# Regrouping the first phase of a fused attention and GEGLU kernel: transposes a slot ahead, stores deferred to SP, more buffers, first fills overlapped

## Chip, cores, metric

One core of one Trainium2 chip. The metric is device time of a whole execution in microseconds (us); lower is better. "Faster" or "slower" means by more than 2%. Of one core there are no sister cores to compare with, so a run counts as slow only if it lies 1.5% above the fastest of its kernel; no run quoted with a ratio did, and the state of a single run is unknown. Marks inside an execution are read from its trace, in us from its start.

## The reference, cut to what matters

```python
x = A_x                                            # 1 x 2048 x 1024, bf16
g = sigmoid((x * gate_w).sum(-1, keepdims=True))   # one gate value for each row
# a: 64 segments of 32 rows; each sees 8 memory rows as well; 40 rows in all
for s in range(64):
    h = concat([mem, x[:, 32*s:32*s+32]])
    q, k, v = h @ Wq, h @ Wk, h @ Wv               # 32 heads of 128
    o = softmax(mask(q k^T * scale)) v ;  o = o @ Wo
    mem = o[:, :8]; outs.append(o[:, 8:])           # the first 8 go to the next segment, 32 are output
# b: GEGLU over all rows
b = gelu(x @ w_gate) * (x @ w_up) @ w_down         # 1024 -> 3584 -> 1024
return g * a + (1 - g) * b
```

The 64 segments depend on one another through `mem`. b doesn't depend on them.

## The kernel before

A list of operations is recorded, and each waits on semaphores for what it reads or overwrites. Five engines work: TensorE (PE), ScalarE (ACT), VectorE (DVE), GpSimd (POOL) and SP, which only issues transfers. A transfer belongs to a "lane", a semaphore; two transfers of one lane are issued one after the other's landing.

**First phase.** 16 tiles of x, 128 rows each, are transposed, kept for products with the first four of 28 gate/up column blocks, and stored to scratch for later. Each "slot" has the products of one column block and the transposes of one tile:

```python
xr = al("xr", [128, TB, KC, 4, NB])                # one buffer
def do_x(T):                                       # tile T; a block is 4 tiles, tb = T % 4
    ... 8 transposes of px[T % 4] into PSUM bank 6 + T % 2
    act: two copies  xTp[fb % 2] <- PSUM
    dve: xr[:, tb] <- PSUM                          # last 8 rows of each segment
    pool: gp <- px * gwb ;  dve: dl[:, T] <- sum(gp)
    if tb == TB - 1:                                # at once, on ACT
        op("act", dma xq_scr <- xTp, lane=f"xw{fb % 2}")
        op("act", dma xr_scr <- xr,  lane="xv")
...
more(4)                                             # four weight slots
for T in range(TB): do_x(T); load_x(T + NPX)
for fb in range(NFB):
    for j in range(NJP):
        pre_j(fb, j)                                # 2 x 8 products, gelu; the last also stores g on ACT
        T = TB * (fb + 1) + j
        if T < NT: do_x(T); load_x(T + NPX)
        more(2)                                     # two more weight slots
more(99)
... gal = 1 / (1 + exp(-dl))
for u in range(2):                                  # late slots: their memory was xTp, wgp, gpre ...
    for m in "vo": ... first((m, u, i))
```

**Weights.** 52 SBUF slots of 512 KB hold the 64 pieces into which Wq, Wk, Wv and Wo are cut. Twelve of them are shared by two pieces and are refetched in every segment when the last use is past. All weight loads stand in SP's one order.

**First fills.** "Fills" compute k, q and v of the last 8 rows of four segments at once ("tails"). Eight of them precede or lie inside segment 0:

```python
def fill0(m, u, b, n, G=0, h=hR):
    for f in fill(m, u, b, h): f()                  # 32 products, all 8 pieces of the weight
    fill_evac(m, u, b, stage[n])                    # ACT copies PSUM
    if m != "v": fill_trans(); fill_put(stage[n], "dve")
    fill_store(m, u, G, stage[n])                   # GpSimd: qk_scr (lane "fq") or v_scr
# in segment 0, in the places named:
#   k,0: fill0 k 0, q 0 (G=0), k 0, q 0 (G=1, hR1)   v,0: fill0 v 0
#   v,0 step 4: load_qk(0, 0); rest_k(0); load_v     k,1: fill0 k 1, q 1, v 1; load_qk(0, 1); load_v; load_r(1)
```

load_qk brings the tails of segment 0 back from qk_scr, load_r(1) brings hR for the second group. After segment 0 come 63 more segments and the rest of the GEGLU.

## Time and profile before

| | us |
|---|---|
| median of 4 runs | 2257.8 (2256.4 to 2265.1) |
| span of the trace | 2259.6 |
| first phase over (last gate/up product) | 113.7 |
| last of the first fills ends | 153.9 |
| segment 0 ends (transposes of a_bf) | 175.6 |

The profile page has the busy digits of 40 equal slices of the span; a view by stretches sums each engine's busy time in stretches that one chooses, with the granted TensorE clock (PEclk), the mean busy share of the 16 DMA engines and the GB/s that they moved. A line of waits has: who waited, for whom, us in total, times, the longest. A line of a timeline has: start, duration, engine, line, operation, operands, count, and in brackets the idle time ahead of it and what ended that. The lines themselves are in the prediction.

### The profile page before, as it was taken

Reading aid. Unit: us, or ns where it says so; the run is one execution under the profiler, and the core shown is the slowest. Engines: PE = TensorE matmul, PEld = TensorE weight load, DVE = VectorE, ACT = ScalarE, POOL = GpSimd, SP = SyncE. Lnnn points to the kernel's source line nnn. Section 1 sums busy time; section 2 is a strip of 40 time slices with the busy share of each in tenths; the row PEclk is TensorE's granted clock in tenths of the full one; section 3 lists DMA queues with packets and bytes.
Section 4 is the critical chain, followed back from the end, with each engine's and each line's share of the span. In section 5 each row is a group of like instructions: output and inputs, shape, how many; then the busy total and the mean of one; then the engine's idle time right before and its main releaser. Section 6 shows DMA issues by size and latency. Waiting matters only on the chain.

```text
span 2259.6 us, 80049 instructions
## 1 busy us (share of the span) xinstructions
PE 2083.4 (92%) x36642; PEld 1098.8 (49%) x36642; DVE 905.4 (40%) x2151; ACT 612.1 (27%) x1296; POOL 618.3 (27%) x1138
## 2 busy tenths in 40 slices
PE   6668999999999999999999989999888999999999
PEld 3324455555545555555555545555543444444444
DVE  4523344334334334334334433433434516344362
ACT  3312223223232323323222232322222303122130
POOL 4223332433433243342333334233321000000000
PEclk9889999999999999999999999999999999999999
DMA  8777888788788888778878878888889500100000
GB/s 288 294 267 269 286 288 296 263 297 307 266 281 300 286 284 316 275 269 316 289 266 295 305 258 286 307 280 283 294 285 342 214 28 29 38 24 33 19 29 19
DMA packets 203536, 529.24 MB, mean 234 GB/s; under 512 B 29640, under 2 KB 46664, under 8 KB 203200
## 3 DMA queue, kind: packets, MB, share of 16 engines
q1 hardware_dynamic: 169264, 464.59, 57.5%
q0 software_dynamic: 28992, 51.94, 7.4%
q10 hardware_dynamic: 4944, 7.60, 0.9%
q8 instruction: 287, 4.70, 0.8%
q14 instruction: 49, 0.40, 0.1%
HBM read 490.36 MB, written 33.55 MB: 232 GB/s over the span
## 4 chain that ended last, share of the span: by engine, by line
PE 76%; DMA 12%; POOL 4%; issue 4%; DVE 2%; ACT 1%; SPq 0%; ACTq 0%; DVEq 0%; POOLq 0%
PE pb L734 24%; PE pb L440 16%; PE pb L746 8%; PE pb L1047 7%; PE pb L761 7%; PE pb L646 4%; DMA sl<-in_A_Wo_dram 3%; DMA sl<-in_A_Wv_dram 3%; PE pb L776 3%; DMA a_scr<-a_bf 2%; PE pb L667 2%; DMA xr_scr<-xr 1%; POOL v_scr L802 1%; PE pb L661 1%; DMA sl<-in_A_Wk_dram 1%
## 5 line engine op out<-in xcount | busy, mean ns | idle before, releaser
L734 PE MATMUL pb<-sl,hT 128*32 128x512 bf16 x12288 | 749.4, 382 | 28.0 <-issue 13.8
L734 PEld LDWEIGHTS pb<-sl,hT 128*32 128x32 bf16 x12288 | 331.7, 97 | 294.7 <-issue 26.7
L746 PE MATMUL pb<-sl,oT 128*32 128x256 bf16 x8192 | 280.3, 275 | 48.7 <-issue 42.8
L634 ACT ACTIVATE tok<-pb 128x512 bf16<-128x512 f32 x320 | 191.0, 597 | 414.7 <-PE pb L734 365.0
L719 POOL COPY oRc<-oT 128x128 bf16<-128x128 bf16 x128 | 97.9, 765 | 647.0 <-DVE oT L637 624.0
L746 PEld LDWEIGHTS pb<-sl,oT 128*32 128x32 bf16 x8192 | 207.8, 97 | 96.9 <-issue 53.2
L761 PE MATMUL pb<-sl,hR 128*32 128x512 bf16 x3072 | 228.0, 385 | 7.5 <-DMA hR<-xr_scr 3.0
L440 PE MATMUL pb<-xT,wg 128*128 128x512 bf16 x768 | 182.8, 381 | 4.1 <-DMA wg<-in_B_w_gate_dram 4.1
L440 PE MATMUL pb<-xT,wu 128*128 128x512 bf16 x768 | 181.4, 379 | 0.0
L1047 PE MATMUL pb<-wd,GT 128*128 128x512 bf16 x784 | 169.9, 379 | 0.0
L637 DVE CAST oT<-pb 128x160 bf16<-128x160 f32 x256 | 71.0, 319 | 220.2 <-PE pb L710 219.7
L634 ACT ACTIVATE vA<-pb 128x512 bf16<-128x512 f32 x128 | 76.4, 597 | 273.9 <-PE pb L734 273.9
L428 ACT ACTIVATE s<-pb 128x512 f32<-128x512 f32 x112 | 66.9, 597 | 307.2 <-PE pb L440 307.1
L637 DVE COPY kT<-pb 128x512 bf16<-128x512 bf16 x128 | 51.8, 405 | 233.5 <-PE pb L646 88.8
L646 PE MATMUL pb<-ident,tok 128*128 128x128 bf16 x1280 | 127.6, 222 | 17.4 <-DVE stg L637 5.7
L646 PEld LDWEIGHTS pb<-ident,tok 128*128 128x128 bf16 x1280 | 72.9, 98 | 127.6 <-ACT tok L634 95.4
L429 DVE SCALAR_TENSOR_TENSOR tp<-s,pb 128x512 f32<-128x512 f32 x112 | 76.8, 685 | 133.3 <-ACT s L428 132.9
L672 DVE TENSOR_REDUCE st<-pb 128x8 f32<-128x320 f32 x128 | 62.9, 492 | 148.1 <-PE pb L667 148.1
L440 PEld LDWEIGHTS pb<-xT,wg 128*128 128x128 bf16 x768 | 75.3, 98 | 95.6 <-issue 6.2
L1047 PEld LDWEIGHTS pb<-wd,GT 128*128 128x128 bf16 x784 | 76.7, 98 | 92.5
L440 PEld LDWEIGHTS pb<-xT,wu 128*128 128x128 bf16 x768 | 75.1, 98 | 90.7 <-issue 0.2
L994 POOL DMA_DIRECT2D out_dram<-osb x14 | 7.6, 547 | 372.4 <-PE pb L440 224.6
(86 smaller groups left out, 2149.7 us busy)
## 6 DMA issues: line engine op xcount, KB each, us to landing
sl<-in_A_Wv_dram SPq DMA_DIRECT2D x394, 512.0 KB, 8.8
sl<-in_A_Wo_dram SPq DMA_DIRECT2D x205, 512.0 KB, 6.0
sl<-in_A_Wk_dram SPq DMA_DIRECT2D x142, 512.0 KB, 5.5
sl<-in_A_Wq_dram SPq DMA_DIRECT2D x79, 512.0 KB, 6.8
qk_scr<-stg POOLq DMA_DIRECT2D x64, 128.0 KB, 5.9
qkr<-qk_scr POOLq DMA_DIRECT2D x128, 64.0 KB, 2.2
wd<-in_B_w_down_dram SPq DMA_DIRECT2D x7, 1024.0 KB, 14.6
px<-in_A_x_dram SPq DMA_DIRECT2D x16, 256.0 KB, 5.2
```

The lines of the kernel that those rows point to most:

```text
L428: op("act", lambda e: e.activation(s1[:, :], hg, ACTF.Square, scale=SQ), rd=[BK(bg)], wr=[s1.r()])
L429: op("dve", lambda e: e.scalar_tensor_tensor(out=t[:, :], in0=s1[:, :], scalar=1.0, in1=hg, op0=ALU.add, op1=ALU.mult), rd=[BK(bg), s1.r() ...
L440: ins = e.matmul(PB[bk][:, 0:FB], lhsT=w[:, kc, cc:cc + 128], rhs=x[:, :, :, kc, :].rearrange("p t i c -> p (t i) c"), start=(kc == 0), st ...
L634: op("act", lambda e: e.activation(o, i, ACTF.Copy), rd=rd, wr=wr)
L637: op("dve", lambda e: e.tensor_copy(o, i), rd=rd, wr=wr)
L646: ins = e.transpose(PBV[TT][:, j * 128:(j + 1) * 128], tok[:, j * 128:(j + 1) * 128], ident[:, :])
L719: op("pool", lambda e: e.tensor_copy(oRc[:, u, :, :].rearrange("p c x -> p x c"), oT[:, :, :, 32:40].rearrange("p g j c -> p (g j) c")), r ...
L734: ins = e.matmul(PB[bk][32 * g:32 * g + 32, :], lhsT=h[:, i, :], rhs=w[:, g * 512:(g + 1) * 512], start=(p % 8 == 0), stop=(p % 8 == 7))
L746: ins = e.matmul(PB[XO][32 * g:32 * g + 32, 0:256], lhsT=oT[:, gp_, 2 * jj + hh, 0:32], rhs=w[:, c:c + 256], start=(r == 0 and p % 8 == 0 ...
L761: ins = e.matmul(PB[b][32 * g:32 * g + 32, :], lhsT=h[:, k[2], :], rhs=w[:, g * 512:(g + 1) * 512], start=(n == 0), stop=(n == 7))
L776: ins = e.matmul(PB[b][32 * g:32 * g + 32, 0:256], lhsT=t[:, :, 2 * i + hh], rhs=w[:, c:c + 256], start=(ends[0] and i == 0 and hh == 0), ...
L1047: ins = e.matmul(PB[bank[2 * k + hf]][:, :], lhsT=GT[:, j, tb * 128:(tb + 1) * 128], rhs=w[:, jj, hf * 512:(hf + 1) * 512], start=(j == 0) ...
```

## The change

The intent is to take the stalls out of the first phase and the first fills. Stores are issued a slot later on SP; xr has two buffers; the first gate/up weights are two tiles each, and their second halves are asked for behind two more x tiles; transposes go ahead of the products; three weight slots are asked for at each step instead of two; late slots are asked for as their memory comes free; first fills overlap with one another, and the tails of segment 0 are copied on chip (they are still stored as well, for segments 1 to 3).

```diff
-        wgp = al("wgp", [128, KC, NJP * 128])
+        wgp = [al(f"wgp{h}", [128, KC, NJP * 64]) for h in range(2)]       # wup likewise
-        xr = al("xr", [128, TB, KC, 4, NB])
+        xr = [al(f"xr{i}", [128, TB, KC, 4, NB], at=(cur[0], xr1)[i]) for i in range(2)]
+        tokB = al("tokB", [128, 512], at=oT.off)
+        st0 = stage + [al(f"st0{i}", [128, 512], at=odd0 + 1024 * i) for i in range(2)]
...
             if j == NJP - 1:      # and the xq_scr and xr_scr stores of do_x likewise
-                op("act", lambda e: e.dma_start(g_scr[fb], ...), lane=f"gw{fb % 2}")
+                puts.append(lambda: op("sp", lambda e: e.dma_start(g_scr[fb], ...), lane=f"gw{fb % 2}"))
...
         for fb in range(NFB):
             for j in range(NJP):
-                pre_j(fb, j)
                 T = TB * (fb + 1) + j
+                now, puts[:] = list(puts), []
                 if T < NT:
                     do_x(T)
                     load_x(T + NPX)
-                more(2)
+                more(3)
+                if T >= NT:
+                    more_late(2 if j < 3 and not inits else 0)
+                for f in now:
+                    f()
+                pre_j(fb, j)
...
         def fill(m, u, b, h=hR):
-            ks = [(m, u, i) for i in range(8)]
+            ks = [(m, u, i) for i in range(8) if i not in PAIRS[m]] + [(m, u, i) for i in PAIRS[m]]
...
+        def tr0(m, u, t, n, G=0):
+            op("pe", lambda e: trans4(e, t), ...)
+            fill_put(st0[n], "dve")
+            if G == 0:            # the tail of segment 0, on chip
+                op("pool", lambda e: e.tensor_copy(qkr[:, u, 0 if m == "q" else 1, :], st0[n][:, 0:128]), ...)
+            fill_store(m, u, G, st0[n])
...              # segment 0
-                on("k", 0, 0, lambda: fill0("k", 0, F1, 0))    # ... and the others one by one
+                on("k", 0, 0, lambda: mm0("v", 0, F1, st0[3]))
+                on("k", 0, 0, lambda: mm0("k", 0, F2, tokB))
+                on("q", 0, 0, lambda: mm0("q", 0, F1, tokB), lambda: more_late(4))
+                on("k", 1, 0, fills_1)
+                on("k", 1, 0, lambda: op("dve", lambda e: e.tensor_copy(hR[:, :, :], hR1[:, :, :]), ...))
+                on("k", 1, 0, lambda: (load_v(0, slice(1, 2)), more_late(99)))
```

More of the change, by code (lines that the diff above doesn't have):

```diff
@@ L406, in bass_gated_mix__memory_aug_recurrent_mem_tr__geglu_ffn__prompt_kernel @@
         NPX = min(NT, 4)
-        xTp = [al(f"xTp{i}", [128, TB, 4, KC, SEG]) for i in range(2)]
-        wgp = al("wgp", [128, KC, NJP * 128])
-        wup = al("wup", [128, KC, NJP * 128])
-        gpre = [al(f"gpre{i}", [128, NJP, FB]) for i in range(2)]
         px = [al(f"px{i}", [128, D]) for i in range(NPX)]
+        gp = al("gp", [128, D], FP32)
         pm = al("pm", [128, D])
         gwb = al("gwb", [128, D])
-        gp = al("gp", [128, D], FP32)
-        dl = al("dl", [128, NT], FP32)
+        xTp = [al(f"xTp{i}", [128, TB, 4, KC, SEG]) for i in range(2)]
+        wgp = [al(f"wgp{h}", [128, KC, NJP * 64]) for h in range(2)]
+        wup = [al(f"wup{h}", [128, KC, NJP * 64]) for h in range(2)]
+        gpre = [al(f"gpre{i}", [128, NJP, FB]) for i in range(2)]
         memT = al("memT", [128, 64])
+        xr1 = cur[0]
+        cur[0] += 2 * TB * KC * 4 * NB
         assert cur[0] <= top
@@ L420, in bass_gated_mix__memory_aug_recurrent_mem_tr__geglu_ffn__prompt_kernel @@
         s1 = al("s1", [128, FB], FP32)
-        xr = al("xr", [128, TB, KC, 4, NB])
+        xr = [al(f"xr{i}", [128, TB, KC, 4, NB], at=(cur[0], xr1)[i]) for i in range(2)]
+        cur[0] += xr[0].nb
+        tokB = al("tokB", [128, 512], at=oT.off)
+        st0 = stage + [al(f"st0{i}", [128, 512], at=odd0 + 1024 * i) for i in range(2)]
+        dl = al("dl", [128, NT], FP32, at=stage[1].off + stage[1].nb - 64)
+        assert cur[0] <= dl.off
         hR1 = al("hR1", [128, KC, 32], at=pB.off)
-        assert cur[0] <= pB.off and hR1.nb <= pB.nb
+        assert hR1.nb <= pB.nb
         hT = hTs[0]
@@ L447, in pre_j @@
             for bk, w in ((bg, wgp), (bu, wup)):
-                up(w, xTp[fb % 2], bk, 128 * j)
+                up(w[2 * j // NJP], xTp[fb % 2], bk, 128 * (j % (NJP // 2)))
             g = gpre[fb % 2]
@@ L451, in pre_j @@
             if j == NJP - 1:
-                op("act", lambda e: e.dma_start(g_scr[fb], g[:, :, :].rearrange("p j c -> p (j c)")), rd=[g.r()],
-                   wr=[("D", "g", fb)], lane=f"gw{fb % 2}")
+                puts.append(lambda: op("sp", lambda e: e.dma_start(g_scr[fb], g[:, :, :].rearrange("p j c -> p (j c)")), rd=[g.r()],
+                                       wr=[("D", "g", fb)], lane=f"gw{fb % 2}"))
+        puts = []
         def load_g(fb):
@@ L472, in do_x @@
             x, n = xTp[fb % 2], 4 * KC * SEG
+            xo_ = xr[fb % 2]
             def f(e):
@@ L481, in do_x @@
             op("act", lambda e: e.activation(x[:, tb, 2:4, :, :], pv[:, 2:4], ACTF.Copy), rd=[BK(b)], wr=[x.r(tb * n + n // 2, tb * n + n)])
-            op("dve", lambda e: e.tensor_copy(xr[:, tb, :, :, :], PBV[b].rearrange("p (k i c) -> p k i c", k=KC, i=4)[:, :, :, NR:SEG]),
-               rd=[BK(b)], wr=[xr.r(256 * tb, 256 * tb + 256)])
+            op("dve", lambda e: e.tensor_copy(xo_[:, tb, :, :, :], PBV[b].rearrange("p (k i c) -> p k i c", k=KC, i=4)[:, :, :, NR:SEG]),
+               rd=[BK(b)], wr=[xo_.r(256 * tb, 256 * tb + 256)])
             op("pool", lambda e: e.tensor_tensor(out=gp[:, :], in0=t[:, :], in1=gwb[:, :], op=ALU.mult),
@@ L486, in do_x @@
             if T < 2:
-                op("pool", lambda e: e.tensor_copy((hR, hR1)[T][:, :, :], xr[:, tb, :, :, :].rearrange("p k i c -> p k (i c)")),
-                   rd=[xr.r(256 * tb, 256 * tb + 256)], wr=[(hR, hR1)[T].r()])
+                op("pool", lambda e: e.tensor_copy((hR, hR1)[T][:, :, :], xo_[:, tb, :, :, :].rearrange("p k i c -> p k (i c)")),
+                   rd=[xo_.r(256 * tb, 256 * tb + 256)], wr=[(hR, hR1)[T].r()])
             op("dve", lambda e: e.tensor_reduce(dl[:, T:T + 1], gp[:, :], AX.X, ALU.add), rd=[gp.r()], wr=[dl.r(T, T + 1)])
             if tb == TB - 1:
-                op("act", lambda e: e.dma_start(xq_scr[TB * fb:TB * fb + TB].rearrange("t p i c -> p t (i c)"),
-                                                x[:, :, :, :, :].rearrange("p t i k c -> p t (i k c)")), rd=[x.r()],
-                   wr=[("D", "xq", y) for y in range(TB * fb, TB * fb + TB)], lane=f"xw{fb % 2}")
-                op("act", lambda e: e.dma_start(xr_scr[TB * fb:TB * fb + TB].rearrange("t p c -> p t c"),
-                                                xr[:, :, :, :, :].rearrange("p t k i c -> p t (k i c)")), rd=[xr.r()],
-                   wr=[("D", "xr", y) for y in range(TB * fb, TB * fb + TB)], lane="xv")
+                puts.append(lambda: op("sp", lambda e: e.dma_start(
+                    xq_scr[TB * fb:TB * fb + TB].rearrange("t p i c -> p t (i c)"), x[:, :, :, :, :].rearrange("p t i k c -> p t (i k c)")),
+                    rd=[x.r()], wr=[("D", "xq", y) for y in range(TB * fb, TB * fb + TB)], lane=f"xw{fb % 2}"))
+                puts.append(lambda: op("sp", lambda e: e.dma_start(
+                    xr_scr[TB * fb:TB * fb + TB].rearrange("t p c -> p t c"), xo_[:, :, :, :, :].rearrange("p t k i c -> p t (k i c)")),
+                    rd=[xo_.r()], wr=[("D", "xr", y) for y in range(TB * fb, TB * fb + TB)], lane=f"xv{fb % 2}"))
         def load_h(s):
@@ L522, in bass_gated_mix__memory_aug_recurrent_mem_tr__geglu_ffn__prompt_kernel, with load_pre @@
             load_x(T)
-        for h in range(2):
-            for w, W, nme in ((wgp, B_w_gate, "gp"), (wup, B_w_up, "up")):
+        def load_pre(h):
+            for w, W, nme in ((wgp[h], B_w_gate, "gp"), (wup[h], B_w_up, "up")):
                 c0, c1 = h * NJP * 64, (h + 1) * NJP * 64
-                op("sp", lambda e, w=w, W=W, c0=c0, c1=c1: e.dma_start(w[:, :, c0:c1], W[:, c0:c1].rearrange("(kc p) c -> p kc c", p=128)),
+                op("sp", lambda e, w=w, W=W: e.dma_start(w[:, :, :], W[:, c0:c1].rearrange("(kc p) c -> p kc c", p=128)),
                    wr=[w.r()], lane=f"{nme}{h}")
+        load_pre(0)
         inits = [k for k in [at_step(p, 0) for p in range(24)] + [(m, 1, i) for m in "kqv" for i in range(8)]
@@ L534, in more, with more_late @@
             del inits[:n]
-        more(4)
+        late = [k for k in [(m, u, i) for u in range(2) for m in "vo" for i in range(8)]
+                if home[k] >= spare and uses[home[k]][0] == k]
+        late.sort(key=lambda k: home[k])
+        def more_late(n):
+            for k in late[:n]:
+                first(k)
+            del late[:n]
         op("pe", tr_mem, rd=[pm.r(), ident.r()], wr=[BK(5)])
@@ L545, in bass_gated_mix__memory_aug_recurrent_mem_tr__geglu_ffn__prompt_kernel @@
                    rd=[xTp[0].r(0, KC * SEG)], wr=[hT.r()])
+            if T == 1:
+                load_pre(1)
+        more(4)
         for fb in range(NFB):
             for j in range(NJP):
-                pre_j(fb, j)
                 T = TB * (fb + 1) + j
+                now, puts[:] = list(puts), []
                 if T < NT:
@@ L552, in bass_gated_mix__memory_aug_recurrent_mem_tr__geglu_ffn__prompt_kernel @@
                     load_x(T + NPX)
-                more(2)
-        more(99)
-        op("act", lambda e: e.activation(gal[:, :], dl[:, :], ACTF.Exp, scale=-1.0), rd=[dl.r()], wr=[gal.r()])
-        op("dve", lambda e: e.tensor_scalar(out=dl[:, :], in0=gal[:, :], scalar1=1.0, scalar2=None, op0=ALU.add),
-           rd=[gal.r()], wr=[dl.r()])
-        op("dve", lambda e: e.reciprocal(gal[:, :], dl[:, :]), rd=[dl.r()], wr=[gal.r()])
-        for u in range(2):
-            for m in "vo":
-                for i in range(8):
-                    if home[m, u, i] >= spare:
-                        first((m, u, i))
+                if T == NT:
+                    op("act", lambda e: e.activation(gal[:, :], dl[:, :], ACTF.Exp, scale=-1.0), rd=[dl.r()], wr=[gal.r()])
+                    op("dve", lambda e: e.tensor_scalar(out=dl[:, :], in0=gal[:, :], scalar1=1.0, scalar2=None, op0=ALU.add),
+                       rd=[gal.r()], wr=[dl.r()])
+                    op("dve", lambda e: e.reciprocal(gal[:, :], dl[:, :]), rd=[dl.r()], wr=[gal.r()])
+                more(3)
[4 more added lines that the diff above has]
+                pre_j(fb, j)
+        for f in puts:
+            f()
+        more(99)
+        more_late(8 - len(hosts) + spare + len(late))
         cur[0] = res0
@@ L642, in evac, with trans4 @@
             act_copy(t[:, :], PB[bank][:, :], [BK(bank)], [t.r()])
-        def trans4(e):
+        def trans4(e, t=tok):
             for j in range(4):
-                ins = e.transpose(PBV[TT][:, j * 128:(j + 1) * 128], tok[:, j * 128:(j + 1) * 128], ident[:, :])
+                ins = e.transpose(PBV[TT][:, j * 128:(j + 1) * 128], t[:, j * 128:(j + 1) * 128], ident[:, :])
             return ins
@@ L808, in fill_store, with mm0 @@
                    rd=[st.r()], wr=[("D", "qk", G, m4)], lane="fq")
-        def fill0(m, u, b, n, G=0, h=hR):
+        def mm0(m, u, b, t, G=0, h=hR):
             for f in fill(m, u, b, h):
                 f()
-            fill_evac(m, u, b, stage[n])
-            if m != "v":
-                fill_trans()
-                fill_put(stage[n], "dve")
-            fill_store(m, u, G, stage[n])
+            act_copy(t[:, :], PB[b][:, :], [BK(b)], [t.r()])
+            if m == "v":
+                fill_store(m, u, G, t)
+        def tr0(m, u, t, n, G=0):
+            op("pe", lambda e: trans4(e, t), rd=[t.r(), ident.r()], wr=[BK(TT)])
+            fill_put(st0[n], "dve")
+            if G == 0:
+                x = 256 * u + 128 * (m == "k")
+                op("pool", lambda e: e.tensor_copy(qkr[:, u, 0 if m == "q" else 1, :], st0[n][:, 0:128]), rd=[st0[n].r(0, 128)],
+                   wr=[qkr.r(x, x + 128)])
+            fill_store(m, u, G, st0[n])
         def rest_k(r):
@@ L853, in bass_gated_mix__memory_aug_recurrent_mem_tr__geglu_ffn__prompt_kernel @@
             if s == 0:
-                on("k", 0, 0, lambda: fill0("k", 0, F1, 0))
-                on("q", 0, 0, lambda: fill0("q", 0, F1, 1))
+                on("k", 0, 0, lambda: mm0("v", 0, F1, st0[3]))
+                on("k", 0, 0, lambda: mm0("k", 0, F2, tokB))
                 if NG > 1:
-                    on("k", 0, 0, lambda: fill0("k", 0, F2, 1, 1, hR1))
-                    on("q", 0, 0, lambda: fill0("q", 0, F2, 0, 1, hR1))
-                on("v", 0, 0, lambda: fill0("v", 0, F1, 1))
@@ L860, in bass_gated_mix__memory_aug_recurrent_mem_tr__geglu_ffn__prompt_kernel @@
-                on("v", 0, 4, lambda: (load_qk(0, 0), rest_k(0), load_v(0, slice(0, 1))))
-                on("k", 1, 0, lambda: fill0("k", 1, F1, 0))
-                on("k", 1, 0, lambda: fill0("q", 1, F2, 1))
-                on("k", 1, 0, lambda: fill0("v", 1, F1, 0))
-                on("k", 1, 0, lambda: (load_qk(0, 1), load_v(0, slice(1, 2)), load_r(1) if NG > 1 else None))
+                    on("k", 0, 0, lambda: mm0("k", 0, F1, tok, 1, hR1))
+                    on("k", 0, 4, lambda: tr0("k", 0, tok, 1, 1))
@@ new lines, in bass_gated_mix__memory_aug_recurrent_mem_tr__geglu_ffn__prompt_kernel, with q_next @@
+                on("k", 0, 0, lambda: tr0("k", 0, tokB, 0))
+                on("q", 0, 0, lambda: mm0("q", 0, F1, tokB), lambda: more_late(4))
+                if NG > 1:
+                    def q_next():
+                        for f in fill("q", 0, F2, hR1):
+                            f()
+                        tr0("q", 0, tokB, 2)
+                        act_copy(tokB[:, :], PB[F2][:, :], [BK(F2)], [tokB.r()])
+                    on("q", 0, 0, q_next)
+                    on("q", 0, 3, lambda: tr0("q", 0, tokB, 3, 1))
+                else:
+                    on("q", 0, 3, lambda: tr0("q", 0, tokB, 2))
@@ new lines, in bass_gated_mix__memory_aug_recurrent_mem_tr__geglu_ffn__prompt_kernel, with fills_1 @@
+                on("v", 0, 4, lambda: (rest_k(0), load_v(0, slice(0, 1))))
+                def fills_1():
+                    mm0("k", 1, F1, tok)
+                    for f in fill("q", 1, F2):
+                        f()
+                    tr0("k", 1, tok, 1)
+                    act_copy(tok[:, :], PB[F2][:, :], [BK(F2)], [tok.r()])
+                    mm0("v", 1, F1, st0[2])
+                    tr0("q", 1, tok, 3)
+                on("k", 1, 0, fills_1)
+                if NG > 1:
+                    on("k", 1, 0, lambda: op("dve", lambda e: e.tensor_copy(hR[:, :, :], hR1[:, :, :]), rd=[hR1.r()], wr=[hR.r()]))
```

## The prediction

> **What bounds the kernel now.** I first read the page's 40 slices. TensorE is over 90% busy in nearly every slice after the third, and the change touches nothing there but the order of eight products inside a fill. What can be won lies in the first three or four slices of 56.5 us:
>
> ```profile
> PE   6668999999999999999999989999888999999999
> PEclk9889999999999999999999999999999999999999
> DMA  8777888788788888778878878888889500100000
> ```
>
> Next I asked for the busy times of the stretches that the code suggests. 0 to 113.6 us is the first phase (x transposed, 16 pairs of gate/up products, stores to scratch); 113.6 to 153.8 us ends with the last of the eight first fills; at 175.6 us the first of 64 segments ends (the two transposes of a_bf):
>
> ```profile
> core 0: us, PE busy (x) PEld busy (x) DVE busy (x) ACT busy (x) POOL busy (x), PEclk, DMA share, GB/s
> 0.00:20.00 20.00, 8.98 (x51) 4.90 (x52) 6.04 (x12) 7.40 (x11) 12.43 (x25) 1.00 0.82 255
> 20.00:113.60 93.60, 68.62 (x342) 31.52 (x340) 47.34 (x71) 30.89 (x55) 25.51 (x12) 0.87 0.82 297
> 113.60:153.80 40.20, 26.08 (x386) 10.45 (x385) 5.20 (x12) 5.77 (x11) 7.57 (x12) 0.90 0.94 350
> 153.80:175.60 21.80, 18.75 (x414) 9.22 (x411) 8.16 (x22) 6.76 (x16) 9.58 (x19) 0.87 0.35 106
> 175.60:199.10 23.50, 20.65 (x476) 10.98 (x476) 9.57 (x27) 6.35 (x16) 6.21 (x13) 1.00 0.81 293
> ```
>
> The reader should see two things. TensorE idles and runs under its full clock up to 153.8 us, though a later segment takes only 23.5 us. But the last two columns show the DMA engines 82% and 94% busy, so there is far less slack in transfers than in TensorE. Third, the waits up to 180 us name the stalls of the first phase; fourth, TensorE's timeline shows one of them whole:
>
> ```profile
> DVE xr L482 <- DMA xr_scr<-xr: 19.3, 3, 12.3
> ```
>
> ```profile
> 78.10 1.89 PE L440 MATMUL pb<-xTp,wup 128*128 128x512 bf16 x8
> 86.34 1.03 PE L476 MATMUL pb<-ident,px 128*128 128x128 bf16 x8 [6.35 <-DVE xr L482]
> 90.16 3.59 PE L440 MATMUL pb<-xTp,wgp 128*128 128x512 bf16 x8 [2.79 <-DVE gpre L434]
> 93.55 2.36 PE L440 MATMUL pb<-xTp,wup 128*128 128x512 bf16 x8
> ```
>
> VectorE can't refill the single xr buffer until its store has landed; TensorE then waits for VectorE, cools down, and its next eight products take 3.59 us in place of 1.89.
>
> **What the Trainium skill says.** "TensorE: Matmul & The Clock Gate", "What's actually happening": the array falls to half its clock after an idle window of about 3.4 us. The lines above agree (3.59 against 1.89 us after the gap). "DMA: Bandwidth & Descriptors", "Issuing engines are not separate DMA queues": transfers issued by SP, ACT or GpSimd run on the same 16 engines, and another issuer saves only sequencer time. So moving stores from ACT to SP buys no bandwidth; this trace agrees in so far as share and GB/s rise and fall together whichever queue works. The same page, "Specifications", gives some 358 GB/s of HBM for a core and 435 for the fabric. This trace had 414 GB/s in 72 to 96 us with weights alone, so the measurement decides: the lower figure is not the ceiling here, the upper one is nearly reached.
>
> **The change part by part.**
>
> 1. Two xr buffers, and stores one slot later on SP. This takes away the 19.3 us of VectorE waiting for xr stores, and frees ACT, which held its own copies back behind stores.
>
> 2. Each x tile is transposed a slot before the products that it follows now, and the first weights are in separate halves. The first product waits for half of the weights (SP's waits show the first halves there at 9.9 and 11.4 us), not until 13.8 and 18.9 us. The three waits of TensorE for ACT's xTp copies (11.9 us together) go.
>
> What compute alone would allow: in the good stretches of the first phase VectorE's slot is xr 0.2, dl 1.2, three products 0.7 each and a tanh of 0.65 between: 4.03 us by the timeline (37.05 to 33.02). TensorE's slot is 0.45+2x1.73 = 3.9 us. The first gelu waits for the chain of gp (2.12) and dl (1.21) of tiles 0 to 4, five times about 3.45 after 6.1 us, so it ends near 26 us. Eleven more slots of 4.1 us give 71; then four slots without x at TensorE's 3.46: the first phase would end near 82 to 85 us rather than 113.6.
>
> 3. The first fills. Order is changed, evacuations overlap other fills, and the tails of segment 0 are copied on chip, so that no qk_scr round trip is waited for (4.3 us of GpSimd waiting for qkr); hR for group 1 is a copy (3.0 us of TensorE waiting for hR). Eight fills of 1.74 us are still to be done, and segment 0.
>
> 4. The o and late v slots are asked for as their memory comes free. In the trace SP issues nothing from 88.8 to 113.7 us (its waits: 17.2 us put to an xq_scr store, then 7.7 us to gate/up products that still read the memory), and the DMA engines fall idle: 35 GB/s in 104 to 108 us, 0 in 108 to 112, 77 in 112 to 116.
>
> **Why the sum is not the sum of the waits.** Count the bytes in SP's new order, in MB (a slot is 512 KB, 0.524 MB). Up to about 20 us: the first eight x tiles 2.1, gate/up weights 2.1, gate_w 0.3, others: 4.7. From there to the end of the last fill (v, second half, which needs refetched v slots): x 2.1; 49 first slots 25.7; refetches of 2 k, 1 q and 6 v slots 4.7; four sets of stores of 1.05+0.26+0.52, 7.3; instructions and small scratch transfers some 1.2: **41 MB**. Every one of them is in front of the refetched v slots in SP's queue. Before moved 297x93.6 + 350x40.2 = 41.9 MB for it, in 0.82x93.6+0.94x40.2 = 114.5 us of full DMA share: 0.366 MB per us of busy engine. Weights alone reach 0.414. With share near 1 and somewhat better packets in flight I take 0.383: 41/0.383 = 107 us, so the last fill ends near 20+107 = **127 us**. Compute alone would be there near 103 (85, plus eight fills 14, plus three stages of projection 5). So transfers become the bound, and 127 replaces 153.8.
>
> From there to the end of segment 0 before took 21.8 us. This path stays nearly as it is: four v_scr stores on GpSimd, the wait for them, the load of vB, then pB, and only then the second part of attention (vB's issue came 5.8 us after the last fill before). The hR wait that goes lies beside that. I take 21 us: segment 0 ends at 148 in place of 175.6, **28 us less**. The later segments are chained on TensorE and their refetches begin at their own uses, so I take the shift through whole, and nothing more: 2258.3 - 28 = **2230 us**.
>
> **The rivals.**
>
> A. Compute sets the first phase after all: stalls vanish and transfers keep up. Segment 0 would end near 121 us, 54 us less, about 2204. For it: TensorE, VectorE and GpSimd have much idle time there. Against it: it asks 41 MB of DMA by about 100 us, 0.51 MB per us, and no window of this trace exceeds 0.42.
>
> B. FIFO behind weights. SP now carries x tiles, stores and three slots per step in one order, so block 1's stores (on which tile 12's xTp and xr wait) come to stand behind backlog. I get these stores landing at 20+14.4/0.383 = 58 us against a need at 53: 5 us of stall, hidden by the DMA bound. Were the rate 0.33, the last fill would end at 144: a gain near 10, about 2248. For it: single windows with stores show 224 to 265 GB/s. Against: their share is then 0.76 to 0.85, so the engines were not full.
>
> C. GpSimd's lane of six qk_scr stores, each waiting for the one before (5.6 us landing plus 0.8 issue, 38 us), is in front of kT's tail copy and the vB loads. If fills end early, it would bind: started near 92 us it ends near 130, just at the fills. It could cost 3 to 5 us.
>
> D. A shift absorbed later: segment 1 shows waits for Wv (0.9 us twice), so later segments nearly run on DMA (0.79 share over all). If any of their waits were on a transfer of fixed time, part of the gain would be lost. I see none; the refetch follows its use.
>
> **Range and chances.** Rates of 0.36 to 0.41 put the last fill at 134 to 120 us: 21 to 35 us of gain. Adding 3 us for the scatter of runs (2256 to 2265) and C gives 2218 to 2243. Over 2% faster needs 45 us, which needs more than the greatest rate seen: 4%. Slower by 2% has no mechanism: 1%.
>
> **What would show it.** Right: DMA share of 0.95 or more from 20 to 120 us without the hole at 104 to 116; no wait of VectorE for xr stores of any size; first phase over near 85 to 90 us; then TensorE waiting for slots of Wk, Wq and Wv in the fills of the second half, ending near 127; a_bf transposes near 148; segments after it at 23 to 26 us as before. Wrong: last fill ahead of 115 us (rival A), a share well under 0.9 with engines waiting on each other (B or C), or segments after the first that differ by more than 0.2 us each, which over 63 would outweigh all of this.

## The result

The changed kernel is correct and took 2230.74 us (median of 4 runs, 2223.8 to 2240.9) against 2257.8. A ratio is the mean time of one kernel's fast runs over that of the other's in the same rounds, so it isn't quite the ratio of these medians: 0.9877, with a 95% interval of 0.983 to 0.9925. A longer comparison later (6 runs against 11 of before) gave 2228.5 against 2265.7 us, ratio 0.9851 (0.9817 to 0.9885). By medians that is 27 and 37 us: faster beyond the noise, by less than 2%.

The same slices of the page of the changed kernel:

```profile
PE   7889999999899899999999899999888999999999
PEclk9989999999999999999999999999999999999999
DMA  9977887788788778878887788788779410000000
```

The view by stretches, cut at its own marks:

```profile
core 0: us, PE busy (x) PEld busy (x) DVE busy (x) ACT busy (x) POOL busy (x), PEclk, DMA share, GB/s
0.00:20.00 20.00, 10.82 (x74) 6.87 (x75) 5.91 (x11) 8.48 (x13) 12.40 (x25) 1.00 0.78 211
20.00:93.00 73.00, 62.13 (x323) 28.75 (x325) 47.20 (x73) 29.23 (x54) 25.54 (x12) 0.93 1.03 393
93.00:127.30 34.30, 25.71 (x383) 10.39 (x383) 4.35 (x9) 5.56 (x10) 7.79 (x14) 0.84 1.03 399
127.30:146.20 18.90, 17.69 (x414) 9.42 (x414) 8.73 (x24) 6.71 (x16) 9.19 (x19) 0.94 0.40 131
```

From 20 us to the last fill the mean share of the DMA engines is 1.03, at 393 and 399 GB/s (before: 0.82 and 0.94, 297 and 350). The work of TensorE in the first fills didn't shrink (25.7 us, before 26.1). TensorE's timeline shows its waits: the first two lines are the longest two after 60 us in the first phase; the rest, from 118 us on, are waits of the first fills for weight slots, 8.6 us in all with those left out here, which is the whole idle time of that stretch:

```profile
61.31 0.88 PE L485 MATMUL pb<-ident,px 128*128 128x128 bf16 x8 [4.84 <-DVE dl L498]
84.24 2.52 PE L446 MATMUL pb<-xTp,wgp 128*128 128x512 bf16 x8 [2.42 <-DVE gpre L440]
118.45 0.62 PE L785 MATMUL pb<-sl,hR 128*32 128x512 bf16 x4 [5.05 <-DMA sl<-in_A_Wq_dram]
...
126.66 0.62 PE L785 MATMUL pb<-sl,hR 128*32 128x512 bf16 x4 [0.69 <-DMA sl<-in_A_Wv_dram]
...
146.25 0.40 PE L992 MATMUL pb<-ident,a_bf 128*128 128x128 bf16 x2
```

| mark, us | before | forecast | changed |
|---|---|---|---|
| first phase over | 113.7 | 82 to 90 | 93.0 |
| last first fill ends | 153.9 | 127 | 127.3 |
| segment 0 ends | 175.6 | 148 | 146.25 |
| span of the trace | 2259.6 | | 2236.0 |

### The profile page after: what moved, and what is told of

The parts are those of the page before. It is cut to its first block, busy times and chain, and to the rows that moved or that the text cites. A ratio compares the mean times of both kernels' runs of the same rounds, so it can differ in the third digit from the quotient of the medians.

```text
span 2236.0 us, 80061 instructions
## 1 busy us (share of the span) xinstructions
PE 2082.7 (93%) x36642; PEld 1097.3 (49%) x36642; DVE 905.4 (40%) x2152; ACT 611.3 (27%) x1296; POOL 616.0 (28%) x1139
## 4 chain that ended last, share of the span: by engine, by line
PE 77%; DMA 11%; issue 4%; POOL 4%; DVE 1%; ACT 1%; SPq 1%; DVEq 0%; POOLq 0%; ACTq 0%
PE pb L758 25%; PE pb L446 15%; PE pb L770 9%; PE pb L1098 8%; PE pb L785 7%; PE pb L670 4%; DMA sl<-in_A_Wo_dram 3%; PE pb L800 3%; DMA sl<-in_A_Wv_dram 3%; DMA a_scr<-a_bf 2%; PE pb L691 2%; PE pb L685 1%; POOL v_scr L826 1%; PE pb L1080 1%; PE pb L724 1%
## 5 line engine op out<-in xcount | busy, mean ns | idle before, releaser
L770 PEld LDWEIGHTS pb<-sl,oT 128*32 128x32 bf16 x8192 | 207.7, 97 | 100.8 <-issue 52.9
L670 PEld LDWEIGHTS pb<-ident,tok 128*128 128x128 bf16 x1268 | 72.2, 98 | 113.7 <-ACT tok L658 86.0
```

The source lines that it names most:

```text
L670: ins = e.transpose(PBV[TT][:, j * 128:(j + 1) * 128], t[:, j * 128:(j + 1) * 128], ident[:, :])
L770: ins = e.matmul(PB[XO][32 * g:32 * g + 32, 0:256], lhsT=oT[:, gp_, 2 * jj + hh, 0:32], rhs=w[:, c:c + 256], start=(r == 0 and p % 8 == 0 ...
```

## The experiments

My theory: from 20 us to the end of the last first fill the changed kernel is bound by what SP's order has in front of the refetched v slots; removing stalls paid only as far as it filled holes in the DMA engines. The rivals: the start is bound by compute; one part (buffers, order of transposes and products, late slots, fills) is nearly all of the gain; or GpSimd's chain of small stores sets the time. The marks of all runs, with the changed kernel twice so that the repeat of a mark can be seen. The last fill and segment 0 repeat to 0.3 us there. The first phase repeats less well: the changed kernel (twice), e3, e7 and e10 have the same first phase, and it ended between 91.0 and 93.0 us:

| run | first phase | last fill | segment 0 | total, us (median, runs) |
|---|---|---|---|---|
| before | 113.7 | 153.9 | 175.6 | 2257.8 (4) |
| changed | 93.0 | 127.3 | 146.25 | 2230.7 (4) |
| e0_after, changed again | 92.4 | 127.6 | 146.1 | 2228.5 (6) |
| e1_more_bytes | 92.8 | 131.0 | 149.6 | 2234.5 (1) |
| e2_less_vector | 88.6 | 124.7 | 143.0 | 2229.0 (1) |
| e3_four_behind | 91.1 | 120.2 | 145.0 | 2232.0 (4) |
| e4_o_behind | 90.4 | 118.4 | 147.6 | 2233.1 (4) |
| e5_late_undone | 90.7 | 131.6 | 151.0 | 2231.9 (1) |
| e6_before_xr2 | 100.8 | 141.5 | 164.0 | 2241.9 (4) |
| e7_fills_undone | 91.0 | 127.25 | 152.9 | 2236.0 (1) |
| e8_one_xr | 111.2 | 140.3 | 161.8 | 2250.9 (1) |
| e9_products_first | 88.8 | 126.3 | 145.4 | 2225.7 (1) |
| e10_two_lanes | 92.2 | 120.5 | 143.2 | 2228.7 (6) |
| e11_early_weights | 90.0 | 118.4 | 141.2 | 2231.9 (5) |

Totals scatter by 8 to 12 us either way and can't separate kernels that differ by 5 us at the start; the marks can. Before too differs between groups of rounds (its medians are 2257.8, 2264.7, 2265.3 and 2265.7), so a total stands against before of its own rounds. All kernels but e2 gave correct results.

**The yardstick (e0_after).**

> The changed kernel itself, once more and longer, as the yardstick for the other runs of this call and for how far the marks of one trace repeat: first phase over at 91 to 93 us, last fill at 127 within 1 us, segment 0 at 146 within 1 us, total 1.2% under before.

Held; the total was 1.5% under before and not 1.2% (ratio 0.9851).

**More bytes, no more compute (e1).**

```diff
+                puts.append(lambda: op("sp", lambda e: e.dma_start(g_two[fb], g[...]), rd=[g.r()], ..., lane=f"gx{fb % 2}"))
```

> The changed kernel with every g store issued twice on SP (the second copy to a scratch that nobody reads): 4 x 0.52 = 2.1 MB more in the same queue, no compute added. Transfer-bound theory: 2.1 MB at the 0.407 MB/us that the changed kernel shows from 40 to 120 us is 5.2 us, so the last first fill ends near 132.4 (127.2 in the changed kernel) and segment 0 (a_bf transposes) near 151 (146.3). Rival, compute-bound start: the last fill stays at 127 within 1 us.

The last fill ended 3.7 us later (131.0 against 127.3) and segment 0 3.3 us later. Compute alone would have given nothing, so bytes do set the mark, but 1.5 us of the expected 5.2 are missing. They can be accounted for: from 20 us to its own last fill e1 moved 44.1 MB at 398 GB/s, the changed kernel 42.4 at 395. So some 1.75 MB more had moved by the mark, not 2.1, and at a slightly higher rate; each is worth some 0.8 us. There is one trace of e1.

**Less compute, the same bytes (e2; wrong on purpose).**

```diff
-            op("dve", lambda e: e.tensor_reduce(dl[:, T:T + 1], gp[:, :], AX.X, ALU.add), ...)
+            if T == 0: op("dve", lambda e: e.memset(dl[:, :], 0.01), wr=[dl.r()])
```

> The changed kernel without the 16 reduces of dl (16 x 1.21 = 19 us of VectorE taken away; the output gate is wrong on purpose). Transfer-bound theory: VectorE's slot falls from 4.0 to 2.8 us and the chain of gp and dl at the start gets shorter, so SP asks for x tiles some 3 us earlier; the last fill comes 0 to 3 us earlier (124 to 127). Rival, VectorE-bound first phase: 11 slots x 1.2 = 13 us or more earlier, last fill near 114.

19 us of VectorE taken away moved the end of the first phase by 4.4 us and the last fill by 2.6, inside what the transfer theory allows for the earlier asking (240 GB/s in the first 20 us instead of 211, then 379 instead of 354 up to 40 us: 1.1 MB, or 2.7 us at 0.4 MB per us). So VectorE is not the bound of the changed kernel's start, though it paces a slot when nothing else holds it up.

**Four o slots behind the refetches (e3).**

```diff
-                on("q", 0, 0, lambda: mm0("q", 0, F1, tokB), lambda: more_late(4))
+                on("q", 0, 0, lambda: mm0("q", 0, F1, tokB))      # more_late(99) at k,1 asks for them
```

> The changed kernel with four o slots (2.1 MB) asked for behind the refetched q and v slots rather than ahead of them. Transfer-bound theory: q's and v's refetches land 5.2 us earlier if they can be issued by then, so the last fill ends near 122 to 123 (127.2), segment 0 near 142 (146.3); total 4 us less than the changed kernel. Rival, compute-bound or set by the time at which the refetches may be asked for (SP issues v's at 108.5 us): last fill stays within 1 us.

The last fill came 7.1 us earlier, at 120.2 (122 to 123 was expected; 2.7 MB less had moved by then, not 2.1): order in the queue decides, and no compute kept it at 127. But segment 0 ended only 1.3 us earlier, a miss of 3 us. A new wait took the gain, on TensorE's timeline of this run:

```profile
132.65 0.24 PE L734 MATMUL pb<-tB,vB 32*128 32x64 bf16 x4 [5.07 <-DMA vB<-v_scr]
```

GpSimd issues that load of vB, and its own timeline in the changed kernel shows what stands in front: qk_scr stores on one lane, each waiting for the landing of the one before.

```profile
112.02 0.76 POOL L831 DMA_DIRECT2D qk_scr<-st  x1 [5.47 <-DMA qk_scr<-stg]
118.40 0.75 POOL L831 DMA_DIRECT2D qk_scr<-st  x1 [5.61 <-DMA qk_scr<-st]
...
124.75 0.76 POOL L831 DMA_DIRECT2D qk_scr<-stg  x1 [4.33 <-DMA qk_scr<-st]
128.22 2.18 POOL L826 DMA_DIRECT2D v_scr<-st  x4 [2.70 <-ACT st L658]
```

In the changed kernel the chain is done at 125.5 us, 2.7 us before the v_scr stores can go; with the last fill 7 us earlier it is too late. This is rival C of the prediction, just below the surface. GpSimd's timeline in e3 itself:

```profile
122.92 0.77 POOL L831 DMA_DIRECT2D qk_scr<-stg  x1 [4.24 <-DMA qk_scr<-st]
123.68 2.19 POOL L826 DMA_DIRECT2D v_scr<-st  x4
...
130.60 0.55 POOL L522 DMA_DIRECT2D vB<-v_scr  x1 [0.31 <-DMA v_scr<-st]
```

The lane is only a part of it. From the first v_scr store to the load of vB took 6.9 us here against 4.6 in the changed kernel (128.22 to 132.80), and the DMA engines were 68% busy in that time against 25%: the o slots that were moved behind the refetches now run beside these small stores. That this is why the stores land later is not tested alone.

**All late o slots behind the refetches (e4).**

```diff
-                    more_late(2 if j < 3 and not inits else 0)
+                    more_late(2 if j == 0 else 0)
...
-        more_late(8 - len(hosts) + spare + len(late))
```

(and the edit of e3)

> As the last one, but all 13 late o slots (6.8 MB) behind the refetches. Transfer-bound theory: up to 10 o slots fewer ahead of the v refetch, 5.2 MB or 13 us, so the last fill would be bound by compute near 113 to 118; but the o slots then come last and o's first half waits for them (near 127 to 131), segment 0 ends between 137 and 142. Rival: as in the last one, no change of the last fill, and o's wait makes segment 0 later than 146.

The last fill came at 118.4, just beyond the upper end of what was expected; segment 0 at 147.6, not 137 to 142: a miss. The wait for vB was 7.7 us here, and DMA share fell to 0.88 in 100 to 120 us, since the refetches can't be asked for before their slots were used (SP waited 12.4 us for the products that still read them, between 85 and 120 us). Putting too much behind opens a hole.

**Late slots asked for only at the end (e5).**

```diff
-                    more_late(2 if j < 3 and not inits else 0)
...
-        more_late(8 - len(hosts) + spare + len(late))
+        more_late(99)
```

(and the edit of e3)

> The changed kernel with all 15 late v and o slots asked for only when the first phase is over, as before. Transfer-bound theory: the queue still has some 3 MB of other work when the first phase ends, so there is at most a short gap, and the last fill has one to three slots more in front of it: 128 to 132 (127.2). Rival, the early asking is what closed the hole of before: a hole of 5 us or more opens at 93 us, last fill at 135 or later.

Last fill at 131.6, segment 0 at 151.0, so 4.8 us of the 29.4 gained are lost. The last fill lies in the range expected, and not at the rival's 135. DMA share fell only to 0.97 in 80 to 100 us, but that small hole is most of the loss: 42.6 MB had moved from 20 us to the last fill, hardly more than the 42.4 of the changed kernel, at 382 GB/s and not 395, and 92 to 96 us had only 281. The slower rate makes some 3.7 of the 4.3 us (42.4 MB at either rate). With all late slots ahead of k's refetch, the wait appears at one slot of Wk, 11.94 us:

```profile
120.58 0.62 PE L783 MATMUL pb<-sl,hR 128*32 128x512 bf16 x4 [11.94 <-DMA sl<-in_A_Wk_dram]
```

**The second xr buffer alone, on the kernel before (e6).**

```diff
-        xr = al("xr", [128, TB, KC, 4, NB])
+        xr = [al(f"xr{i}", [128, TB, KC, 4, NB], at=(None, xr1)[i]) for i in range(2)]
...
-                   ..., lane="xv")
+                   ..., lane=f"xv{fb % 2}")
```

> The kernel before with a second xr buffer (and a second lane for its store) and nothing else. Its xr waits of VectorE were 19.3 us. Transfer-bound theory: the first phase ends near 97 (113.7) and the hole behind it closes with it, but the bytes then set the pace: last fill near 140 (153.9), segment 0 near 161 (175.6), 14 us gained. Rival, the waits add up: segment 0 at 156. Rival, the other waits take its place (late first weights, ACT held by its stores): 170 or later.

The first phase was over at 100.8, segment 0 at 164.0: 11.6 us gained of 29.4, from 19.3 us of waits removed (14 were expected). DMA share still fell to 0.82 and 0.91 in 20 to 40 and 100 to 120 us. Its total gave 0.9873 (0.9818 to 0.9928), a larger gain than the marks show: 11.6 us alone would be 0.9949, outside the interval. The marks say what the edit did to the start; what else made these totals differ from before's is not explained.

**One xr buffer in the changed kernel (e8).**

```diff
-            xo_ = xr[fb % 2]
+            xo_ = xr[0]                               # and lane="xv"
```

> The changed kernel with one xr buffer again, the deferred stores kept. Each of three blocks must then wait on VectorE for an xr store that stands behind some 10 us of weights in SP's queue: first phase ends 20 to 30 us later (113 to 123 against 93.0), SP, which waits for x tiles in order, leaves holes, last fill near 140 to 150. Rival, the stall is hidden by the transfers anyway: last fill at 127 to 130.

First phase over at 111.2, last fill at 140.3, segment 0 at 161.8: 15.5 us of the gain are lost. VectorE's wait is back, and longer than the 19.3 us of before:

```profile
DVE xr L491 <- DMA xr_scr<-xr: 29.1, 3, 10.3
```

The buffer and the deferral belong together: here a store that stands behind weights in one queue needs the second buffer all the more.

**First fills as before (e7).**

```diff
-                on("k", 0, 0, lambda: mm0("v", 0, F1, st0[3]))       # ... to fills_1
+                on("k", 0, 0, lambda: fill0("k", 0, F1, 0))          # ... the block of before, with load_qk and load_r(1)
```

> The changed kernel with the first fills as before: each evacuated by itself, tails of segment 0 through qk_scr and back, hR for group 1 loaded. Transfer-bound theory: the last fill still waits for the v refetches and ends at 127 to 130 (127.2); the path from there is the one of before, 21.8 us instead of 19.0, so segment 0 ends near 149 to 152 (146.3). Rival, fills bound by their own chain: the last fill ends at 93 + 40 = 133 as the stretch of 40 us before, segment 0 at 155.

The last fill ended at 127.25, to 0.1 us where it was: overlapping the fills gained nothing there, as they wait for the refetches either way. But from there to the end of segment 0 it took 25.7 us, not 19.0 (21.8 was expected), and TensorE's timeline of this run names 4.6 us of it:

```profile
138.41 1.04 PE L785 MATMUL pb<-sl,hR 128*32 128x512 bf16 x8 [4.64 <-DMA hR<-xr_scr]
```

So the part on the fills, undone here as a whole (order, overlap and on-chip copies), is worth 6.7 us, all of it behind the last fill. The wait for hR makes 4.6 of them; how the rest divides, and why this path is 3.9 us longer than that of before, isn't shown.

**Products ahead of the transposes (e9).**

```diff
+                pre_j(fb, j)
                 if T < NT:
                     do_x(T)
...
-                pre_j(fb, j)
```

> The changed kernel with each step's gate/up products issued ahead of its transposes, as before; all other parts stay. Transfer-bound theory: TensorE and VectorE wait a little more (up to 3 us at each of three block changes, first phase over at 93 to 100), but SP asks for x tiles no more than a few us later and its queue stays full, so the last fill moves by 0 to 3 us (127 to 130). Rival, the order is the main part of the gain: last fill at 135 or later.

All three marks came slightly earlier (88.8, 126.3, 145.4), the first by more than its scatter of 2 us. The order of transposes and products shows no gain once the other parts are there (one trace). I had expected a longer first phase; it was not longer.

**Looking for a better kernel (e10, e11).** e10 is e3 with two lanes for the six first qk_scr stores:

```diff
-                   ..., wr=[("D", "qk", G, m4)], lane="fq")
+                   ..., lane=("fq", "fq2")[(G, u) == (1, 0) or (G, u, m) == (0, 1, "q")])
```

> The kernel with four o slots behind the refetches, whose last fill ended at 120.2 but whose second part of attention then waited 5.1 us for vB, with the six first qk_scr stores on two lanes in turn, so that GpSimd waits for the store before the last and not for the last. Theory, GpSimd's lane took the place of the transfers: the vB wait falls to under 1 us and segment 0 ends at 140 to 141 (145.0 with one lane, 146.3 in the changed kernel); total 4 to 5 us under that, about 6 under the changed kernel. Rival, vB waits for its v_scr store, whatever the lane does: segment 0 stays at 144 to 145.

The wait for vB fell from 5.07 to 2.32 us and segment 0 to 143.2: the lane was half of it, as GpSimd then waited 4.43 us for the landing of the v_scr stores, with the DMA engines 96% busy (121.4 to 129.1 us). Segment 0 at 140 to 141 and a wait under 1 us had been expected: a miss. e11 also asks for two weight slots between x tiles 5 and 6:

```diff
                 load_pre(1)
+                more(2)
-        more(4)
+        more(2)
```

> As e10_two_lanes, with two of the first weight slots (1.05 MB) asked for between the x tiles at 13 us, when the DMA engines carried 211 GB/s, rather than behind them at 19 us. Transfer-bound theory: 1.05 MB moved into idle time is 2.6 us, last fill and segment 0 up to 2.6 us earlier. Rival: x tiles 6 and 7 come later by the same 2.6 us and the first phase with them, or compute now sets the last fill: no gain, or a loss of up to 3 us.

Another 2.0 us, of the 2.6 that 1.05 MB moved into idle time should give at most: 141.2, 5 us ahead of the changed kernel. Neither total shows it: 2228.7 and 2231.9 against 2228.5 in the same rounds. The next 62 segments took 1530.8 and 1527.6 us in these two traces, 1525.0 and 1517.9 in the two of the changed kernel, 1520.8 in that of before and 1514.6 in e9's. Such differences outweigh 5 us.

The profiled run was the slowest of six for e10 and of five for e11, so these traces aren't typical. In two long segments of e10 (28.0 and 27.2 us) the mean granted clock was 0.94, with gaps of up to 1.73 us for which the profile names nothing ("issue"). The clock records of the traces go on from there: over the 62 segments the granted clock of TensorE was 0.5 for 30.7 us in e10 and 27.3 in e11, for 13.7 in before and in both traces of the changed kernel, and for 10.2 in e9. Their DMA records show that each of the 71 "issue" gaps of the changed trace between 180 and 2200 us ended 1.1 to 1.6 us after a 16 KB packet of the instruction queue had landed, each after a different packet; the 75 gaps of e10 and the 60 of e9 look the same. So these gaps look like late instruction fetches, which no run here tests. Whether e11 beats the changed kernel in the total stays open.

## Why the prediction was right

- **Bytes over rate.** Forecast: 41 MB at 0.383 MB per us from 20 us, 107 us. Measured: 395 GB/s over 107.3 us, so 42.4 MB at 0.395. Both terms were 3% low and cancelled; that the time was right to 0.3 us is luck, the mechanism is not. That the mark is made by bytes was shown by e1, e3 and e4 (bytes or their order move it, by 3.7 to 8.9 us) and by e2 (compute hardly does). The same count over the other runs (GB/s of the view by stretches from 20 us to the last fill, times the length) agrees: wherever the late slots stay ahead of the refetches and no store is added (before, the changed kernel twice, e2, e5 to e9), 41.8 to 42.6 MB had moved from 20 us to the last fill. What differed was the rate: 0.312 MB per us before, 0.345 in e6, 0.348 in e8, 0.382 in e5, and 0.390 to 0.399 in the others.
- **Rival A** is excluded: no 20 us of the changed trace exceed 409 GB/s. Nor is one part nearly all of the gain: at segment 0 the second buffer is worth 11.6 us alone and 15.5 with the rest there, the fills 6.7, the late slots 4.8; they overlap and don't add up to the 29.4.
- **Stalls of the first phase.** The xr wait went, as forecast. The first phase ended at 93 and not at 82 to 90. Rival B's estimate was that block 1's stores would land at 58 us against a need at 53; the xq_scr store ended ACT's wait at 58.7. The lines of waits in the changed kernel name this and one that the prediction hadn't counted, g's store with its two buffers:

```profile
ACT xTp L489 <- DMA xq_scr<-xTp: 5.6, 1, 5.6
DVE gpre L440 <- DMA g_scr<-gpre: 4.1, 1, 4.1
```

  Both are new prices of the one queue, and mostly hidden behind the bytes as the prediction said: e9 and e2 ended the phase 2 to 4 us earlier and moved segment 0 by 0.9 and 3.2 us, e2 by asking earlier for bytes.
- **Part 3, the path after the last fill.** Forecast 21 us, measured 19.0. The step "The hR wait that goes lies beside that" was wrong: e7 shows hR's wait (4.64 us) on the path and 6.7 us in all for the fills' part. The error was 2 us, and the trace of before held the answer: hR's 3.0 us are TensorE's only wait there between the last fill and the end of segment 0, and 21.8 less 3.0 is 18.8. For vB, on which the prediction had put the path, TensorE waited only 0.7 us in the changed kernel.
- **Part 4, late slots.** 4.8 us by e5. The hole was closed, but mainly by the backlog that the unstalled phase builds up (share 0.97 without part 4, against the 35 and 0 GB/s of before); what part 4 adds is that no small hole stays at 92 to 100 us.
- **Part 2.** Forecast as an enabler and not priced alone; e9 shows no gain from its order of transposes and products. The first product, which was to start once half of the weights were there, began at 14.33 us against 13.81 before, behind the transposes of a fifth tile, and the second at 17.44 against 18.92. The halved weights, three slots a step for two, and the deferral of stores without a second buffer on the kernel before I didn't try alone.
- **Rival C** was close: the lane of qk_scr stores had 2.7 us to spare (e3).
- **No loss of the shift on the way is seen.** 29.4 us at the end of segment 0, 23.6 us in the spans of the two traces, 27 and 37 us by medians. The differences between are of the size of the scatter of 62 segments, which took 0.07 us more and 0.05 us less each than before's in the two traces, under the 0.2 us that the prediction named as a sign of being wrong. No wait that absorbs the shift was found. That the total met 2230 to within 1 us is luck too, with runs from 2223.8 to 2240.9.

## What to carry to other kernels

Before adding up stalls, add up the bytes that must land before the mark and divide by the best rate of the trace: here, with the queue's order as it was, all parts together could gain what the holes in the DMA engines held and little more. Where one queue carries everything, its order is a schedule: what is needed first goes first, and every deferred store needs buffers for the backlog that it stands behind. Once the bound is met, look at the next chain in line (here GpSimd's serial small stores) before moving work ahead of it, and judge a change of 5 us at marks in the trace if the total scatters by 8, without claiming it for the total.

## What the Trainium skill lacked or had wrong

- "DMA: Bandwidth & Descriptors", "Specifications", gives some 358 GB/s as the HBM limit of a core, without a condition in its table. The changed kernel, a program on one core, held 405 to 409 GB/s for 80 us (40 to 120), loads and stores mixed. The same page says under "Bandwidth" that each core gets about 358 when both cores of an HBM domain stream, and measured 425 for one large load of a single core; the second fits better here.
- The same page, "Anatomy of one DMA — SWDGE (gpsimd) path", fits a transfer of GpSimd as 2.0 us and bytes over 436 GB/s: by that an estimate of 2.3 us for a 128 KB qk_scr store. With the DMA engines full it took 5.6 us (median), and v_scr's 32 KB took 5.5 us. The page says nothing of how the fixed part grows under such a load beyond its remark on HBM latency.
- Instruction fetch belongs to "Runtime: NRT & Kernel Launch", "Instruction fetch mechanics", which has no duration for TensorE's waits on it. The changed trace has 65 us of gaps put to "issue" in 71 waits from 180 us to 2200 us, up to 2.4 us each, all ending 1.1 to 1.6 us after a 16 KB instruction packet landed. That they are fetches is inferred from these times alone.
